# Beginning the first two FFN1 tiles on four pairs between the last score chunks, in a fused sigmoid attention and SwiGLU kernel

## The chip, the cores and the metric

The kernel runs on one core of a Trainium2 chip. The metric is device time in microseconds for one execution.

## The reference, cut to what matters

```python
# q, k, v: (8, 12, 448, 64)
scores = q @ k.T / 8 - log(448)
attn   = sigmoid(scores) @ v                 # "PV"
x      = attn as (3584, 768)
out    = (silu(x @ w_gate) * (x @ w_val)) @ w_out   # FFN1: w_gate, w_val (768, 1536); FFN2: w_out
```

The kernel works on quads of four heads; three quads give the x of one batch. x is held transposed as six "pairs" of 128 rows each (two pairs to a quad), and FFN1 sums over the six pairs. So the first FFN1 tile can be begun on pairs 0 to 3 while the third quad, quad 2, still lacks its last score chunks and its PV.

## The kernel before

Four accumulator tiles of two banks each form a ring; every score chunk, transpose, PV and FFN1 tile takes one. A score chunk is four 64x64 matmuls and one sigmoid on ScalarE (0.89 us from one to the next). FFN1 is one 128x128 matmul for each pair and bank: bank 0 gate, bank 1 value.

```python
def pv(n, how=0, at=None):
    ...                                     # 28 matmuls of 64x64 into P
    first = nc.vector.tensor_copy(out=x, in_=P[:, 0, :S])           # even pair, bank 0
    ...
    halves = [...]                                                  # odd pair, bank 1
    if how == 2:
        for o, i in halves:
            nc.scalar.copy(out=o, in_=i)    # waits for `first`
```

The stretch of the change. The comments give the ring tile by number:

```python
    chunk(2, 3)                             # tile 0
    chunk(2, 4)                             # tile 1, still being read by PV of quad 1
    chunk(2, 5)                             # tile 2

    k0 = ring_at[0] % 4                     # 3
    chunk(2, 6, at=(k0 + 1) % 4)            # tile 0
    early = [Banked("f", at=(k0 + i) % 4) for i in (0, 2)]      # tiles 3 and 1
    ffn1_mm(early[0], 0, 0, range(NP - 2))  # 8 matmuls
    ffn1_mm(early[1], 0, 1, range(2))       # 4
    pv(2, how=2, at=(k0 + 3) % 4)           # tile 2
    ffn1_mm(early[1], 0, 1, range(2, NP - 2))
    early.append(Banked("f", at=(k0 + 1) % 4))
    ffn1_mm(early[2], 0, 2, range(NP - 2))
    for f, Df in enumerate(early):
        ffn1_mm(Df, 0, f, range(NP - 2, NP))        # pairs 4 and 5, of quad 2
        ffn1_gate(Df, 0, f)
```

Of the kernel before, what the change touches and what calls it, by code (L numbers as in the profile page):

```python
# [19 lines left out]
def kernel(  # L20
# [10 lines left out]
    nc = tc.nc  # L31
    ctx.enter_context(tc.manual_schedule())

    B, H, S, D = q.shape
# [4 lines left out]
    NP = H // 2  # L39
# [74 lines left out]
    def apart(second, *firsts):  # L114

        for first in firsts:
            keys[0] += 1
            tc.add_to_no_dep_group(f"half{keys[0]}", first.ins)
            tc.declare_no_dep(second.ins, group=f"half{keys[0]}", reason="another bank or other partitions")


    FW = 3
    NW = NF // FW
    wg16 = [one.tile([128, NP, FW * 128], FP16, tag=f"wg{i}", name=f"wg16_{i}") for i in range(NW)]
    wv16 = [one.tile([128, NP, FW * 128], FP16, tag=f"wv{i}", name=f"wv16_{i}") for i in range(NW)]
# [93 lines left out]
    xT = {}  # L219

    def qk_tile(n, c, at=None):
        sd = Banked(at=at)
        sc = sd.t
        qt, kt = qT[(n, 0)], qT[(n, 1, c)]
        for w in range(2):
            for h2 in range(2):
                r = slice(h2 * 64, h2 * 64 + 64)
                nc.tensor.matmul(  # L228
                    out=sc[w * 64:(w + 1) * 64, h2, :S],
                    lhsT=kt[r, w * 64:(w + 1) * 64],  # L230
                    rhs=qt[r, :, w * 64:(w + 1) * 64],
                    start=True,
                    stop=True,
                )
        return sd

    def sig_tile(n, c, sd, split=False):
        sc = sd.t
        pt = ptp.tile([128, 2, S], FP16, tag="pt", name="pt")
        if split:  # L240
            for h2 in range(2):
                sd.read(
                    nc.scalar.activation(out=pt[:, h2, :], in_=sc[:, h2, :S], func=SIGM, bias=sb_t, scale=qkscale), h2  # L243
                )
        else:
            nc.scalar.activation(out=pt, in_=sc[:, :, :S], func=SIGM, bias=sb_t, scale=qkscale)  # L246
        pts[(n, c)] = pt

    def pv(n, how=0, at=None):

        b, j = divmod(n, NJ)
        P = Banked(at=at).t
        vt = v16.pop(n)
        for c in range(C):
            pt = pts.pop((n, c))
            for h2 in range(2):
                for w in range(2):
                    r = slice(w * 64, w * 64 + 64)
                    g = (w ^ h2) * 64
                    nc.tensor.matmul(  # L260
                        out=P[g:g + 64, h2, :S],
                        lhsT=vt[r, h2, c * D:(c + 1) * D],
                        rhs=pt[r, h2, :],
                        start=(c == 0),
                        stop=(c == C - 1),
                    )

        x = xtp.tile([128, S], FP16, tag="xT", name=f"xT_{b}_{2 * j}")
        first = nc.vector.tensor_copy(out=x, in_=P[:, 0, :S])  # L269
        xT[(b, 2 * j)] = x  # L270
        x = xtp.tile([128, S], FP16, tag="xT", name=f"xT_{b}_{2 * j + 1}")
        xT[(b, 2 * j + 1)] = x
        halves = [(x[w * 64:(w + 1) * 64, :], P[(1 - w) * 64:(2 - w) * 64, 1, :S]) for w in range(2)]
        done = [nc.vector.tensor_copy(out=o, in_=i) for o, i in halves[how:]]  # L274
        if how == 2:
            for o, i in halves:
                nc.scalar.copy(out=o, in_=i)

        def rest():
            if how == 1:  # L280
                o, i = halves[0]
                apart(nc.scalar.copy(out=o, in_=i), first, *done)

        return rest
# [1 line left out]

    hT = {}

    def ffn1_mm(D, b, f, prs):
        cs = slice((f % FW) * 128, (f % FW) * 128 + 128)  # L290
        for i, w16 in enumerate((wg16, wv16)):
            for pr in prs:
                D.write(
                    nc.tensor.matmul(  # L294
                        out=D.t[:, i, :S], lhsT=w16[f // FW][:, pr, cs], rhs=xT[(b, pr)],
                        start=(pr == 0), stop=(pr == NP - 1),
                    ),
                    i,
                )

    def ffn1(b, f):
        D = Banked("f", made=(b // 2, f))
        for prs in (range(NP - 2), range(NP - 2, NP)) if f == 0 else (range(NP),):
            ffn1_mm(D, b, f, prs)
        ffn1_gate(D, b, f)
        if b % 2:
            h_sums(b // 2, f)
            make_sums(2)
# [217 lines left out]
    for grp in visits:  # L526
        n, c = grp[0]
        b, j = divmod(n, NJ)
# [6 lines left out]
    def attn_step(group, pvs, how):  # L535
        for part in (group[:2], group[2:]):
            scs = [(n, c, qk_tile(n, c)) for n, c in part]
            rest = [pv(pvs.pop(0), how) for _ in range(len(pvs))]
            for i, (n, c, sc) in enumerate(scs):

                sig_tile(n, c, sc, split=len(group) == 4 and part[0] == group[0] and i == 1)
            for f in rest:
                f()
# [51 lines left out]
    def chunk(n, c, at=None):  # L595
        sig_tile(n, c, qk_tile(n, c, at))
# [22 lines left out]
    for c in range(3):  # L619
        chunk(1, c)  # L620
    pv(0)
    chunk(1, 3)
    chunk(1, 4)
# [9 lines left out]
    chunk(2, 0)  # L633
    chunk(2, 1)
    pv(1)
    chunk(2, 2)
    trans_pe(3)
# [3 lines left out]
    w_load("g", 3)  # L641
    w_load("v", 3)
    chunk(2, 3)
    chunk(2, 4)
    chunk(2, 5)

    k0 = ring_at[0] % 4
    chunk(2, 6, at=(k0 + 1) % 4)
    early = [Banked("f", at=(k0 + i) % 4) for i in (0, 2)]
    ffn1_mm(early[0], 0, 0, range(NP - 2))  # L650
    ffn1_mm(early[1], 0, 1, range(2))
    pv(2, how=2, at=(k0 + 3) % 4)
    ffn1_mm(early[1], 0, 1, range(2, NP - 2))
    early.append(Banked("f", at=(k0 + 1) % 4))
    ffn1_mm(early[2], 0, 2, range(NP - 2))
    for f, Df in enumerate(early):
        ffn1_mm(Df, 0, f, range(NP - 2, NP))
        ffn1_gate(Df, 0, f)
# [84 lines left out]
```

## Time and profile before

| | before |
|---|---|
| time, median of the first 3 runs | 416.99 us (416.38 to 417.77) |
| span of the profiled run | 415.2 us |
| TensorE busy | 97% |
| the stretch: from the scores of (2,3) to the first scores of the next visit | 21.61 to 34.46 = 12.85 us |
| gaps of TensorE in it | 0.52 and 0.32 us |

The rows of the profile are in the prediction. In a TensorE row, the first number is when the first matmul starts, but the second reaches to the end of the last one in the pipeline, so consecutive rows overlap; distances between starts are the safe reading.

### The profile page before, as it was taken

The numbers are of one execution on the slowest core, as the hardware profiler recorded it, in microseconds if no ns is written. First come the engines' busy times: TensorE is split into PE (matmuls) and PEld (weight loads), VectorE is DVE, ScalarE is ACT, GpSimd is POOL, SyncE is SP. The second block draws the span as 40 slices with busy tenths as digits, with TensorE's granted clock in tenths as the row PEclk, the third lists the DMA queues.
The fourth block names the chain that finished last, engine by engine and source line by source line (L and its number), as shares of the span: only waits on it lengthen the run. The fifth ranks groups of instructions, "written<-read, shape, count | busy, mean of one in ns | idle before, by whom it ended". The sixth has DMA issues, their size and how long they took to land.

```text
span 415.2 us, 7941 instructions
## 1 busy us (share of the span) xinstructions
PE 404.5 (97%) x3194; PEld 210.9 (51%) x3194; DVE 257.1 (62%) x472; ACT 213.4 (51%) x294; POOL 95.0 (23%) x125
## 2 busy tenths in 40 slices
PE   7899999999999999999999999999999999999995
PEld 3444544545555445445565445445555545555563
DVE  3637557779755555678654555568745447578653
ACT  5966985754444745845704865565715472222000
POOL 4528163345130553210030345020000000000000
PEclk9999999999999999999999999999999999999999
DMA  8999999996779995331275998330025400000135
GB/s 267 246 256 242 223 199 250 130 211 173 199 148 231 184 207 157 66 98 24 59 184 139 198 203 209 77 69 0 2 59 140 113 2 0 2 0 2 38 81 148
DMA packets 59845, 54.39 MB, mean 131 GB/s; under 512 B 35744, under 2 KB 53280, under 8 KB 59808
## 3 DMA queue, kind: packets, MB, share of 16 engines
q0 software_dynamic: 18880, 30.94, 34.3%
q1 hardware_dynamic: 40496, 22.62, 25.4%
q8 instruction: 25, 0.41, 0.4%
q10 hardware_dynamic: 432, 0.33, 0.3%
q14 instruction: 12, 0.10, 0.1%
HBM read 47.19 MB, written 11.01 MB: 140 GB/s over the span
## 4 chain that ended last, share of the span: by engine, by line
PE 87%; ACT 5%; DVE 4%; issue 2%; DMA 1%; SPq 0%; DVEq 0%; ACTq 0%
PE ps_D L294 49%; PE ps_D L418 18%; PE ps_D L228 8%; PE ps_D L260 6%; PE ps_D L476 6%; ACT pt L246 4%; DVE t L314 1%; DVE hT L318 1%; DMA st<-in_k_dram 1%; DVE S L377 1%; PE ps_D L198 1%; ACT s L312 0%; ACT pt L243 0%; SPq L149 0%; DVE T L204 0%
## 5 line engine op out<-in xcount | busy, mean ns | idle before, releaser
L246 ACT ACTIVATE pt<-ps_D,sb_t 128x896 f16<-128x896 f32 x148 | 140.2, 1016 | 83.4 <-PE ps_D L228 78.6
L294 PE MATMUL ps_D<-xT,wg 128*128 128x448 f16 x576 | 126.8, 353 | 0.1
L294 PE MATMUL ps_D<-xT,wv 128*128 128x448 f16 x576 | 126.4, 352 | 0.0
L314 DVE TENSOR_TENSOR t<-ps_D,s 128x448 f16<-128x448 f32 x96 | 59.7, 622 | 74.7 <-ACT s L312 74.4
L312 ACT ACTIVATE s<-ps_D 128x448 f16<-128x448 f32 x96 | 52.6, 548 | 83.4 <-PE ps_D L294 71.3
L294 PEld LDWEIGHTS <-wg 128*128 128x128 f16 x576 | 53.5, 98 | 58.3 <-issue 12.4
L294 PEld LDWEIGHTS <-wv 128*128 128x128 f16 x576 | 56.4, 98 | 52.6
L318 DVE SCALAR_TENSOR_TENSOR hT<-ps_D,t 128x448 f16<-128x448 f32 x96 | 60.0, 625 | 10.0
L179 POOL CAST c<-st 128x896 bf16<-128x896 f32 x41 | 38.5, 947 | 120.9 <-DMA T<-c 61.8
L228 PE MATMUL ps_D<-T,T 64*64 64x448 bf16 x644 | 44.2, 357 | 2.2 <-DVE T L204 0.8
L260 PE MATMUL ps_D<-pt,v 64*64 64x448 f16 x672 | 36.0, 349 | 0.4 <-ACT pt L246 0.3
L429 DVE TENSOR_SCALAR osb<-ps_D 128x384 f32<-128x384 f32 x43 | 24.0, 558 | 19.1 <-PE ps_D L418 18.1
L418 PEld LDWEIGHTS <-S 128*128 128x128 f16 x264 | 25.8, 98 | 17.1
L418 PE MATMUL ps_D<-wT,S 128*128 128x384 f16 x198 | 34.0, 326 | 0.0
L228 PEld LDWEIGHTS <-T 64*64 64x64 bf16 x644 | 15.0, 105 | 25.1 <-issue 19.0
L172 POOL DMA_DIRECT2D v<-in_v_dram x24 | 17.6, 731 | 44.3 <-PE ps_D L228 32.9
L269 DVE CAST xT<-ps_D 128x448 f16<-128x448 f32 x24 | 14.9, 622 | 19.7 <-PE ps_D L260 14.3
L435 DVE SCALAR_TENSOR_TENSOR osb<-ps_D,osb 128x384 f32<-128x384 f32 x33 | 18.4, 558 | 13.5 <-PE ps_D L418 13.5
L274 DVE CAST xT<-ps_D 64x448 f16<-64x448 f32 x42 | 26.1, 621 | 0.7
L260 PEld LDWEIGHTS <-v 64*64 64x64 f16 x672 | 19.8, 107 | 13.0 <-issue 1.6
L418 PEld LDWEIGHTS <-hT 128*128 128x128 f16 x198 | 18.9, 98 | 14.2 <-issue 2.1
L476 PE MATMUL ps_D<-wo,hT 128*128 128x384 f16 x144 | 24.2, 326 | 0.0
(45 smaller groups left out, 213.3 us busy)
## 6 DMA issues: line engine op xcount, KB each, us to landing
out_dram<-osb SPq DMA_DIRECT2D x52, 192.0 KB, 3.0
st<-in_q_dram POOLq DMA_DIRECT2D x20, 448.0 KB, 4.9
st<-in_k_dram POOLq DMA_DIRECT2D x20, 448.0 KB, 6.3
v<-in_v_dram POOLq DMA_DIRECT2D x24, 224.0 KB, 7.3
wg<-in_moe_w_gate_dram POOLq DMA_DIRECT2D x4, 576.0 KB, 11.9
wv<-in_moe_w_val_dram POOLq DMA_DIRECT2D x4, 576.0 KB, 13.0
wo<-in_moe_w_out_dram POOLq DMA_DIRECT2D x4, 576.0 KB, 9.8
st<-in_q_dram SPq DMA_DIRECT2D x3, 448.0 KB, 7.1
```

Of the source, the lines that this page charges most:

```text
L179: eng.tensor_copy(out=t.rearrange("p c h d -> p h c d"), in_=st.rearrange("p h (c d) -> p h c d", c=C))
L228: nc.tensor.matmul(out=sc[w * 64:(w + 1) * 64, h2, :S], lhsT=kt[r, w * 64:(w + 1) * 64], rhs=qt[r, :, w * 64:(w + 1) * 64], start=True, st ...
L246: nc.scalar.activation(out=pt, in_=sc[:, :, :S], func=SIGM, bias=sb_t, scale=qkscale)
L260: nc.tensor.matmul(out=P[g:g + 64, h2, :S], lhsT=vt[r, h2, c * D:(c + 1) * D], rhs=pt[r, h2, :], start=(c == 0), stop=(c == C - 1),)
L274: done = [nc.vector.tensor_copy(out=o, in_=i) for o, i in halves[how:]]
L294: nc.tensor.matmul(out=D.t[:, i, :S], lhsT=w16[f // FW][:, pr, cs], rhs=xT[(b, pr)], start=(pr == 0), stop=(pr == NP - 1),),
L312: D.read(nc.scalar.activation(out=s16, in_=D.t[:, 0, :S], func=SIGM), 0)
L314: D.read(nc.vector.tensor_tensor(out=t1, in0=D.t[:, 0, :S], in1=s16, op=MULT), 0)
L318: nc.vector.scalar_tensor_tensor(out=hT[(b // 2, f)][:, b % 2, :], in0=D.t[:, 1, :S], scalar=HSC, in1=t1, op0=MULT, op1=MULT),
L418: nc.tensor.matmul(out=D.t[:, bank, :hw], lhsT=l, rhs=B_(i), start=(first and i == 0), stop=(i == HF - 1), skip_group_check=True,),
L429: nc.vector.tensor_scalar(out=o, in0=D.t[:, bank, :hw], scalar1=HREC, scalar2=None, op0=MULT), bank
L476: nc.tensor.matmul(out=D.t[:, half, :hw], lhsT=h[:, m * 128:(m + 1) * 128], rhs=wo16[f // FW][:, f % FW, half * hw:(half + 1) * hw], start ...
```

## The change

The intent: fill the time in which TensorE waits for the sigmoids of quad 2 with FFN1 work that is ready, and let ScalarE's two PV copies start at once, as PV now has less work behind it to hide them.

```diff
             for o, i in halves:
-                nc.scalar.copy(out=o, in_=i)
+                apart(nc.scalar.copy(out=o, in_=i), first)
 ...
     chunk(2, 3)
-    chunk(2, 4)
-    chunk(2, 5)
     k0 = ring_at[0] % 4
-    chunk(2, 6, at=(k0 + 1) % 4)
-    early = [Banked("f", at=(k0 + i) % 4) for i in (0, 2)]
-    ffn1_mm(early[0], 0, 0, range(NP - 2))
-    ffn1_mm(early[1], 0, 1, range(2))
+    tile_of = lambda i: Banked("f", at=(k0 + i) % 4)
+    four = range(NP - 2)
+    chunk(2, 4, at=(k0 + 1) % 4)
+    early = [tile_of(0)]
+    ffn1_mm(early[0], 0, 0, four, (0,))      # gate only
+    chunk(2, 5, at=(k0 + 3) % 4)
+    ffn1_mm(early[0], 0, 0, four, (1,))      # value only
+    early.append(tile_of(2))
+    ffn1_mm(early[1], 0, 1, four, (0,))
+    chunk(2, 6, at=(k0 + 1) % 4)
+    ffn1_mm(early[1], 0, 1, four, (1,))
     pv(2, how=2, at=(k0 + 3) % 4)
-    ffn1_mm(early[1], 0, 1, range(2, NP - 2))
-    early.append(Banked("f", at=(k0 + 1) % 4))
-    ffn1_mm(early[2], 0, 2, range(NP - 2))
+    early.append(tile_of(1))
+    ffn1_mm(early[2], 0, 2, four)
```

`apart` tells the scheduler that the second instruction need not wait for the first. (`ffn1_mm` also takes a list of banks now; that line is cut.)

More of the change, by code (lines that the diff above doesn't have):

```diff
@@ L287, with ffn1_mm @@
     hT = {}
-    def ffn1_mm(D, b, f, prs):
+    def ffn1_mm(D, b, f, prs, banks=(0, 1)):
         cs = slice((f % FW) * 128, (f % FW) * 128 + 128)
-        for i, w16 in enumerate((wg16, wv16)):
+        for i in banks:
             for pr in prs:
@@ L294, in ffn1_mm @@
                     nc.tensor.matmul(
-                        out=D.t[:, i, :S], lhsT=w16[f // FW][:, pr, cs], rhs=xT[(b, pr)],
+                        out=D.t[:, i, :S], lhsT=(wg16, wv16)[i][f // FW][:, pr, cs], rhs=xT[(b, pr)],
                         start=(pr == 0), stop=(pr == NP - 1),
```

## The prediction

> **What bounds the kernel now.** I read the page first, for the engine shares and the chain that ended last; then the chain in order of time, to see whether the changed stretch (about 20 to 35 us) is on it; then the timelines of TensorE and ScalarE there; then the waits and the DMA issues. The page's chain first:
>
> ```profile
> PE 87%; ACT 5%; DVE 4%; issue 2%; DMA 1%; SPq 0%; DVEq 0%; ACTq 0%
> ```
>
> TensorE is the bound of the kernel as a whole. Time can be won here only where TensorE idles, or where it does more than the arithmetic needs. The TensorE timeline of the changed stretch (start, length, engine, line, operation, what ended the idle time before it):
>
> ```profile
> 20.71 0.94 PE L198 MATMUL ps_D<-idn,c 128*128 128x128 bf16 x14
> 21.61 0.38 PE L228 MATMUL ps_D<-T,T 64*64 64x448 bf16 x4
> 22.52 0.57 PE L228 MATMUL ps_D<-T,T 64*64 64x448 bf16 x8 [0.52 <-DVE xT L274]
> 23.41 0.38 PE L228 MATMUL ps_D<-T,T 64*64 64x448 bf16 x4 [0.32 <-ACT pt L246]
> 23.72 0.93 PE L294 MATMUL ps_D<-xT,wg 128*128 128x448 f16 x4
> ```
>
> L228 is the scores, four matmuls to a chunk. Counting tiles of the ring of four, the row at 21.61 is chunk (2,3), the one at 22.52 is (2,4) and (2,5) together, the one at 23.41 is (2,6). L294 is FFN1 and L260 is PV. There are two gaps, 0.52 and 0.32 us. From 23.41 on TensorE has no gap until about 45 us, as the chain shows (start, length, what):
>
> ```profile
> 22.24 1.13 ACT pt L246
> 23.36 0.04 issue
> 23.41 0.38 PE ps_D L228 x4
> 23.79 2.38 PE ps_D L294 x12
> 26.16 1.45 PE ps_D L260 x28
> 27.61 6.92 PE ps_D L294 x36
> 34.53 0.50 PE ps_D L228 x8
> 35.03 2.38 PE ps_D L294 x12
> ...
> 41.07 0.69 PE ps_D L228 x12
> ```
>
> Before 23.41 the pace is the sigmoid's. The ScalarE timeline holds thirteen of them back to back:
>
> ```profile
> 14.23 11.82 ACT L246 ACTIVATE pt<-ps_D,sb_t 128x896 f16<-128x896 f32 x13
> 28.39 1.06 ACT L277 CAST xT<-ps_D 64x448 f16<-64x448 f32 x2 [2.34 <-DVE xT L269]
> ```
>
> The last begins at 24.91 and ends at 26.05; they start 0.89 apart and last about 1.12 each. Counted back, the sigmoid of (2,2) ends at 22.46, of (2,3) at 23.36, of (2,4) at 24.25, of (2,5) at about 25.15. The second row is the two PV half copies, which begin only after VectorE's copy of the other bank has ended at 28.35.
>
> **What the Trainium skill says.** TensorEngine Tiling (Array Packing), section Key Properties: changing the tiling mode, not just the tile, drains TensorE. Scores and PV run as 64x64 tiles, FFN1 as the full array, so each passage from one to the other should cost something. The trace agrees: full-array blocks of 12 and 36 matmuls take 2.38 and 6.92 us, which is 0.189 each and 0.11 for the block; 64x64 blocks of 8 and 12 take 0.50 and 0.69, which is 0.0475 each and 0.12 for the block (28 then make 1.45, as PV does). TensorE: Matmul & The Clock Gate, section Step-by-step: matmuls stay in program order, only weight loads are pulled ahead; so a chunk that waits blocks the FFN1 work behind it, which is why the order of the program matters here. PSUM — Partial Sum Buffer, section PSUM bank collisions raise a hardware error: two engines on different banks run clean. The DVE copy takes bank 0 of PV's tile and ScalarE's halves take bank 1, so the wait that the change drops is not needed for safety; no run yet shows them side by side in this kernel.
>
> **The change part by part.** No instruction is removed or added: the same three chunks, 24 early FFN1 matmuls, 28 PV matmuls and five copies. What changes is the order on TensorE, the ring tile of each, and one dependency.
>
> Tiles. The start of the local numbering, k0, is now taken after chunk (2,3) instead of after (2,5), so it is ring tile 1 instead of 3. Chunk (2,4) goes to the tile of (2,2) and waits for that sigmoid (22.46), where it had waited for the last VectorE copy of PV of quad 1 (22.46 as well: the copy starts 21.84 and lasts 0.62). With the 0.05 us that other releases show it starts at about 22.51, as before at 22.52. So the first gap, 0.52 us, stays. The first FFN1 tile sits on the tile of that PV and is placed behind (2,4), so it can't fill it either. Chunk (2,5) waits for the sigmoid of (2,3), chunk (2,6) for that of (2,4); both orders keep a two-chunk distance.
>
> Order. I use the two laws above and check them on the kernel before. From 22.52: 8 score matmuls 0.50, to 23.02; wait to 23.41 (0.39); 4 scores 0.31, to 23.72; 12 FFN1 2.38, to 26.10; PV 1.45, to 27.55; 36 FFN1 6.92, to 34.47. The timeline's weight loads start at 23.72, 26.09, 27.54 and 34.46, so the laws hold within 0.01 us.
>
> After, from 22.51: (2,4) 0.31, to 22.82; gate of tile 0 on four pairs, 4 x 0.189 + 0.11 = 0.87, to 23.69; (2,5) 0.31, to 24.00, its sigmoid freed at 23.36, so no wait; eight FFN1 (value of tile 0, gate of tile 1) 1.62, to 25.62; (2,6) 0.31, to 25.93, freed at 24.25, no wait; four FFN1 0.87, to 26.80; PV 1.45, to 28.25; the remaining 32 FFN1 to the same point (eight of tile 2, twelve to close the three tiles, twelve of tile 3) 32 x 0.189 + 0.11 = 6.16, to 34.41.
>
> So the sum is 34.47 - 34.41 = 0.06 us won. Its terms: the gap filled, -0.39; one more score block, +0.12; two more full-array blocks, +0.22; the start, -0.01. The gap is filled, but the interleaving that fills it pays nearly all of it back in mode changes.
>
> ScalarE. Scores of (2,5) come at about 24.07, just where its slot was (24.02). Those of (2,6) come at about 26.0, so the last sigmoid moves from 24.91 to about 26.05 and ends at 27.15. PV needs it only for its last four matmuls, at 26.80 + 0.12 + 24 x 0.0475 = 28.06. Tile 2 of FFN1 on that ring tile comes at 28.25. So ScalarE's lost 1.1 us is off the path.
>
> PV copies. Before, PV's first copy began 0.18 us after the next weight load; so after, VectorE copies from 28.43 to 29.05. FFN1 asks for pair 4 at 28.25 + 0.11 + 8 x 0.189 = 29.87 and for pair 5 at 30.06. The halves on ScalarE take 1.06: in the old way from 29.09 to 30.15, late by about 0.1 to 0.15 us; at once, from 28.45 to 29.51, in time by half a microsecond. The dropped dependency is thus an insurance that the new order needs, not a gain over the kernel before, where the halves ended at 29.45 and were asked for at 30.0.
>
> DMA. The first gate and value weights, issued at 9.58 and 10.41:
>
> ```profile
> wg<-in_moe_w_gate_dram POOLq DMA_DIRECT2D x1, 576.0 KB, 10.3
> wv<-in_moe_w_val_dram POOLq DMA_DIRECT2D x1, 576.0 KB, 12.4
> ```
>
> They land at 19.9 and 22.8. The new order asks for them at 22.8 and 24.0, so neither is waited for.
>
> Downstream of 30 us the order of instructions is that of before, with the ring roles (PV, tile 0, tile 1, tile 2) in the same order, so the shift of 0.06 us should be carried to the end unchanged.
>
> **The rivals.** First: the mode changes are hidden, because the intercepts of my laws are drain that is there only at the end of a long block. Then the whole 0.39 us comes through, and the time would be 416.6. For it: the intent of the change. Against it: PV, between two FFN1 blocks, shows the 0.12 in full (1.45), and the two laws reproduce four block starts of the kernel before. Second: a short block costs more than the line says (I extrapolate from 12 full-array matmuls to 4), or the four-pair blocks meet a wait I haven't seen, such as the T copies of quad 3 that hold tile 1's ring tile (they end at 23.65; asked for at about 24.9) or a dependency of the changed tiles. At 0.1 to 0.3 us more for the three short blocks the time would be 417.1 to 417.3. Third: the first gap too is shortened, if (2,4) is released by the sigmoid a little sooner than by VectorE; by the starts above that is worth under 0.05 us. Fourth: the early sigmoids' new times change what GpSimd issues and when, and with it the later loads; the score chunks' inputs are long there and the chain has DMA only in its first 7 us, so this should be worth nothing.
>
> **Range and chances.** Predicted change -0.06 us, which no timing here resolves: the three runs before spread over 1.4 us (416.38 to 417.77). From the median, 416.99 - 0.06 = 416.9. The rivals reach from 416.6 to 417.3, and a median of a few runs wanders by some 0.4 either way, so I take 416.2 to 417.6 for 8 in 10. Two per cent are 8.3 us, more than the whole changed stretch could lose without an error: faster 0.005, same 0.99, slower 0.005.
>
> **What would show it right or wrong.** In the changed kernel's TensorE timeline there should be no gap after (2,4); the rows should alternate scores 4, FFN1 4, scores 4, FFN1 8, scores 4, FFN1 4, PV 28; PV should start at about 26.8 instead of 26.09, and the first scores of the next visit at 34.4 instead of 34.46. If these come at about 34.1, the mode change was free (first rival); if at 34.7, short blocks cost more (second). The gap before (2,4) should still be about 0.5. The sigmoids should show an idle time of about 1 us before the last, and the ScalarE halves should start with VectorE's copy. I am wrong if TensorE waits inside PV for the last sigmoid, or at FFN1's pair 5 for the halves, or if the time past 34.5 differs between the kernels by more than the shift.

## The result, and the profile after

The changed kernel took 416.60 us in the median of 6 runs (416.14 to 417.43); the kernel before, 416.84 in 6. The ratio is 0.9996, with a 95% interval of 0.9979 to 1.0012: the same. (A ratio is the mean time of one kernel's fast runs over that of the other's in the same rounds, so not quite the ratio of the medians quoted.)

The TensorE timeline of the changed kernel in the stretch; columns as before:

```profile
21.12 0.38 PE L228 MATMUL ps_D<-T,T 64*64 64x448 bf16 x4
22.02 0.38 PE L228 MATMUL ps_D<-T,T 64*64 64x448 bf16 x4 [0.52 <-ACT pt L246]
22.33 0.93 PE L294 MATMUL ps_D<-xT,wg 128*128 128x448 f16 x4
23.19 0.38 PE L228 MATMUL ps_D<-T,T 64*64 64x448 bf16 x4
23.51 0.93 PE L294 MATMUL ps_D<-xT,wv 128*128 128x448 f16 x4
24.27 0.92 PE L294 MATMUL ps_D<-xT,wg 128*128 128x448 f16 x4
25.12 0.38 PE L228 MATMUL ps_D<-T,T 64*64 64x448 bf16 x4
25.44 0.93 PE L294 MATMUL ps_D<-xT,wv 128*128 128x448 f16 x4
26.30 1.52 PE L260 MATMUL ps_D<-pt,v 64*64 64x448 f16 x28
27.75 0.93 PE L294 MATMUL ps_D<-xT,wg 128*128 128x448 f16 x4
```

The alternation: scores 4, FFN1 4, scores 4, FFN1 8, scores 4, FFN1 4, PV 28. One gap is left, 0.52 us before (2,4) at 22.02; the one of 0.32 us is gone. The next visit's scores start at 33.91, so the stretch is 33.91 - 21.12 = 12.79 us against 12.85. The profiled span is 0.5 us shorter than before, but (2,3), which precedes everything that was changed, already started 0.49 us sooner: that part is the scatter of the start, not the change.

ScalarE over the same time:

```profile
17.28 7.41 ACT L246 ACTIVATE pt<-ps_D,sb_t 128x896 f16<-128x896 f32 x8
25.62 1.01 ACT L246 ACTIVATE pt<-ps_D,sb_t 128x896 f16<-128x896 f32 x1 [0.93 <-PE ps_D L228]
27.87 1.06 ACT L277 CAST xT<-ps_D 64x448 f16<-64x448 f32 x2 [1.24 <-PE ps_D L260]
```

The last sigmoid starts after 0.93 us of idle time, and the two half copies start at 27.87, where VectorE's copy starts at 27.94: they lie side by side, and the runs below that keep this (e1, e3, e4, e5) are recorded as correct.

The chain of the changed kernel just behind the stretch (start, length, what) shows what a block costs besides its matmuls. It counts from the end of one block to the end of the next, so it has 33.98 where the timeline has 33.91:

```profile
33.98 0.50 PE ps_D L228 x8
34.48 2.38 PE ps_D L294 x12
36.86 0.50 PE ps_D L228 x8
37.36 0.89 PE ps_D L198 x14
38.25 2.27 PE ps_D L294 x12
40.52 0.69 PE ps_D L228 x12
```

Twelve FFN1 matmuls take 2.38 us behind scores (34.48) but 2.27 us behind the transposes of L198 (38.25). Those transposes use the full array, like FFN1. So the 0.11 us belongs to the passage from 64x64 tiles to the full array and not to "a new block".

What the 0.11 us is made of stays open. TensorE's weight loads (PEld) of the kernel before:

```profile
23.72 0.49 PEld L294 LDWEIGHTS <-wg 128*128 128x128 f16 x4 [0.20 <-issue]
24.30 0.67 PEld L294 LDWEIGHTS <-wv 128*128 128x128 f16 x4
```

The first load of the block starts together with its first matmul (23.72), while inside the block the first value weights are loaded 0.19 us ahead of their matmul (24.49). A load takes about 0.10 us (in the mean 98 ns for the 128x128 loads of L294, 105 and 107 ns for the 64x64 loads of L228 and L260), so a first load that nothing covers would look much like a drain of the array. No run tells the two apart; the cost of a passage is the same whichever it is.

### The profile page after: what moved, and what is told of

The parts are those of the page before. It is cut to its first block, busy times and chain, and to the rows that moved or that the text cites. A ratio compares the mean times of both kernels' runs of the same rounds, so it can differ in the third digit from the quotient of the medians.

```text
span 414.7 us, 7943 instructions
## 1 busy us (share of the span) xinstructions
PE 403.1 (97%) x3194; PEld 209.9 (51%) x3194; DVE 256.7 (62%) x472; ACT 213.5 (51%) x294; POOL 94.5 (23%) x125
## 4 chain that ended last, share of the span: by engine, by line
PE 89%; ACT 4%; DVE 3%; issue 2%; DMA 1%; POOL 0%; SPq 0%; DVEq 0%; ACTq 0%
PE ps_D L294 51%; PE ps_D L418 18%; PE ps_D L228 8%; PE ps_D L260 6%; PE ps_D L476 5%; ACT pt L246 3%; DMA st<-in_q_dram 1%; PE ps_D L198 1%; DVE S L377 1%; DVE t L314 1%; ACT s L312 0%; DVE hT L318 0%; ACT pt L243 0%; DVE T L204 0%; DVE xT L269 0%
## 5 line engine op out<-in xcount | busy, mean ns | idle before, releaser
L294 PE MATMUL ps_D<-xT,wg 128*128 128x448 f16 x576 | 126.6, 353 | 0.1
L294 PE MATMUL ps_D<-xT,wv 128*128 128x448 f16 x576 | 126.3, 352 | 0.0
L294 PEld LDWEIGHTS <-wg 128*128 128x128 f16 x576 | 53.5, 98 | 58.3 <-issue 12.4
L294 PEld LDWEIGHTS <-wv 128*128 128x128 f16 x576 | 56.2, 98 | 52.6 <-issue 0.4
L318 DVE SCALAR_TENSOR_TENSOR hT<-ps_D,t 128x448 f16<-128x448 f32 x96 | 60.0, 625 | 10.0
L228 PE MATMUL ps_D<-T,T 64*64 64x448 bf16 x644 | 44.4, 357 | 2.6 <-DVE T L204 1.2
L260 PE MATMUL ps_D<-pt,v 64*64 64x448 f16 x672 | 36.0, 349 | 0.4 <-ACT pt L246 0.3
L228 PEld LDWEIGHTS <-T 64*64 64x64 bf16 x644 | 15.0, 105 | 25.6 <-issue 19.3
L260 PEld LDWEIGHTS <-v 64*64 64x64 f16 x672 | 19.8, 107 | 13.0 <-issue 1.0
L476 PE MATMUL ps_D<-wo,hT 128*128 128x384 f16 x144 | 24.2, 326 | 0.3 <-DVE osb L489 0.3
```

Source lines behind the costliest of these rows:

```text
L228: nc.tensor.matmul(out=sc[w * 64:(w + 1) * 64, h2, :S], lhsT=kt[r, w * 64:(w + 1) * 64], rhs=qt[r, :, w * 64:(w + 1) * 64], start=True, st ...
L260: nc.tensor.matmul(out=P[g:g + 64, h2, :S], lhsT=vt[r, h2, c * D:(c + 1) * D], rhs=pt[r, h2, :], start=(c == 0), stop=(c == C - 1),)
L294: nc.tensor.matmul(out=D.t[:, i, :S], lhsT=(wg16, wv16)[i][f // FW][:, pr, cs], rhs=xT[(b, pr)], start=(pr == 0), stop=(pr == NP - 1),),
L318: nc.vector.scalar_tensor_tensor(out=hT[(b // 2, f)][:, b % 2, :], in0=D.t[:, 1, :S], scalar=HSC, in1=t1, op0=MULT, op1=MULT),
L476: nc.tensor.matmul(out=D.t[:, half, :hw], lhsT=h[:, m * 128:(m + 1) * 128], rhs=wo16[f // FW][:, f % FW, half * hw:(half + 1) * hw], start ...
```

## The experiments

"Rest" is the span less the end of the stretch, that is, everything behind it.

| run | what | stretch, expected | stretch, measured | rest |
|---|---|---|---|---|
| before | | | 12.85 | 380.7 |
| changed | | 12.79 | 12.79 | 380.8 |
| e1_apart_only | before, halves let loose | 12.85 | 12.85 | 380.6 |
| e2_no_apart | changed, halves wait | 12.9 to 13.05 | 13.04 | 382.6 |
| e3_merged | changed, two passages fewer | 12.56 to 12.66 | 12.79 | 382.0 |
| e4_split1 | changed, two passages more | 13.02 | 13.03 | 381.9 |
| e5_split3 | changed, six passages more | 13.48 | 13.48 | 380.4 |
| e6_one_fill | before, one block moved | 12.70 | 12.71 | 382.4 |
| e7_both_gaps | both gaps filled | 12.20 to 12.5 | 12.31 | 380.7 |
| e8_pairs | e7, (2,5) beside (2,6) | 12.08 | 12.78 | 382.3 |
| e9_wo_later | before, a later load | 12.85 | 12.85 | 380.9 |
| e10_both | e8 and e9 | 12.08 | 12.54 | 382.0 |

### The halves alone, and the order alone

```diff
# e1: kernel before
-                nc.scalar.copy(out=o, in_=i)
+                apart(nc.scalar.copy(out=o, in_=i), first)
# e2: changed kernel
-                apart(nc.scalar.copy(out=o, in_=i), first)
+                nc.scalar.copy(out=o, in_=i)
```

> The kernel before, with only the halves of PV on ScalarE let loose from VectorE's copy. The measure of all these runs is the stretch on TensorE from the four scores of chunk (2,3) to the eight scores of the next visit: 12.85 us before (21.61 to 34.46), 12.79 changed (21.12 to 33.91). Theory (the order of TensorE alone makes the time, the halves are off its path): the halves start with VectorE's copy, some 0.7 us sooner, and the stretch stays 12.85 within 0.03. Rival (the small gain of the change came from the halves): the stretch falls by about 0.05 or more.

Measured: the halves started at 28.33, 0.12 us behind the first FFN1 matmul after PV (28.21), where in the kernel before that distance is 0.84; and the stretch did not move (22.28 to 35.13). Letting them loose alone wins nothing.

> The changed kernel, with the halves waiting for VectorE's copy again. Theory of the prediction: the new order leaves only eight FFN1 matmuls behind PV, so the second of pair 5's halves comes late. From the changed trace the halves would end 28.60 + 1.06 = 29.66, and pair 5 is asked for at 29.46: TensorE waits some 0.15 to 0.25 us at pair 5 and the stretch grows from 12.79 to 12.9 to 13.05, so the change without it would be slower than before in this stretch. Rival (the dropped dependency is no part of the result): the stretch stays 12.79 within 0.03.

Measured: 21.38 to 34.42 = 13.04. TensorE where FFN1 tile 0 asks for pairs 4 and 5, and ScalarE's halves:

```profile
29.54 0.79 PE L294 MATMUL ps_D<-xT,wg 128*128 128x448 f16 x2
30.17 0.54 PE L294 MATMUL ps_D<-xT,wv 128*128 128x448 f16 x2
```

```profile
28.86 1.06 ACT L277 CAST xT<-ps_D 64x448 f16<-64x448 f32 x2 [1.97 <-DVE xT L269]
```

Two such matmuls take 0.54 in every other row; here the pair takes 0.79, so 0.25 us is spent waiting for halves that end at 28.86 + 1.06 = 29.92. The new order needs the dropped dependency: without it the change would cost 0.19 us instead of winning 0.06.

### More passages

```diff
# e4: changed kernel; pv() calls mid[c] ahead of its chunk c
-    ffn1_mm(early[1], 0, 1, four, (1,))
-    pv(2, how=2, at=(k0 + 3) % 4)
+    ffn1_mm(early[1], 0, 1, range(2), (1,))
+    pv(2, how=2, at=(k0 + 3) % 4, mid={3: range(2, 4)})
# e5
+    ffn1_mm(early[1], 0, 1, range(1), (1,))
+    pv(2, how=2, at=(k0 + 3) % 4, mid={2: range(1, 2), 4: range(2, 3), 6: range(3, 4)})
```

> The changed kernel with the four value matmuls of tile 1 split two and two, the second two put after 12 of the 28 matmuls of PV. Same instructions, same tiles, no new wait (the gap of TensorE is already filled, and the last sigmoid ends before PV's last chunk needs it), but two more passages between full-array and 64x64 matmuls. Theory (each passage costs 0.11 to 0.12 us): the stretch grows by 0.23, from 12.79 to 13.02. Rival (passages are free, the constant of a block is an artefact of long blocks or of waits): 12.79 within 0.03.

> As the run before, but the four value matmuls of tile 1 lie singly: one ahead of PV, one after each of its first 8, 16 and 24 matmuls, so six more passages than in the changed kernel. Theory (cost per passage, whatever the length of the block): the stretch grows by 6 x 0.115 = 0.69, from 12.79 to 13.48. Rival a (free): 12.79. Rival b (the line doesn't hold down to blocks of one matmul, a short block costs more): over 13.6.

Measured: 13.03 and 13.48, so 0.24 us for two passages and 0.69 for six, 0.115 to 0.12 each. The TensorE timeline of e5 inside PV:

```profile
25.61 0.36 PE L296 MATMUL ps_D<-xT,wv 128*128 128x448 f16 x1
25.91 0.57 PE L262 MATMUL ps_D<-pt,v 64*64 64x448 f16 x8
26.41 0.36 PE L296 MATMUL ps_D<-xT,wv 128*128 128x448 f16 x1
26.70 0.57 PE L262 MATMUL ps_D<-pt,v 64*64 64x448 f16 x8
27.21 0.36 PE L296 MATMUL ps_D<-xT,wv 128*128 128x448 f16 x1
27.50 0.57 PE L262 MATMUL ps_D<-pt,v 64*64 64x448 f16 x8
```

One full-array matmul between two 64x64 blocks occupies 25.91 - 25.61 = 0.30 us, of which the matmul itself is 0.19; eight PV matmuls occupy 0.50, of which 0.38 is their own. No row shows a wait. The rival that passages are free falls, and so does the one that short blocks cost more than the line says: it holds from 36 matmuls down to one.

### One block moved

```diff
# e6: kernel before
-    chunk(2, 6, at=(k0 + 1) % 4)
-    early = [Banked("f", at=(k0 + i) % 4) for i in (0, 2)]
-    ffn1_mm(early[0], 0, 0, range(NP - 2))
+    early = [Banked("f", at=k0)]
+    ffn1_mm(early[0], 0, 0, range(NP - 2))
+    chunk(2, 6, at=(k0 + 1) % 4)
+    early.append(Banked("f", at=(k0 + 2) % 4))
```

> The kernel before with one move: the eight matmuls of FFN1 tile 0 stand ahead of the scores of (2,6) instead of behind them; tiles as before. The wait before (2,6), 0.39 us, shrinks to about 0.13 (tile 0 now waits for the first T copy of quad 3), and only one more full-array block is made (+0.11, its score block stays single). Theory: the stretch (12.85 before, 12.79 changed) becomes 12.70. Rival (fills are worth their full wait): 12.59. Rival (what is filled is always paid back): 12.85.

Measured: 21.61 to 34.32 = 12.71. A single moved block wins 0.14 us, more than twice what the change wins, with two passages more than the kernel before where the change has four more. So the same gap is worth more with fewer passages, even though 0.15 us of it is left: FFN1 starts at 23.17, where the laws without a wait make 23.02.

### Fewer passages

```diff
# e3: changed kernel
     early = [tile_of(0)]
-    ffn1_mm(early[0], 0, 0, four, (0,))
+    ffn1_mm(early[0], 0, 0, four)
     chunk(2, 5, at=(k0 + 3) % 4)
-    ffn1_mm(early[0], 0, 0, four, (1,))
     early.append(tile_of(2))
-    ffn1_mm(early[1], 0, 1, four, (0,))
+    ffn1_mm(early[1], 0, 1, four)
     chunk(2, 6, at=(k0 + 1) % 4)
-    ffn1_mm(early[1], 0, 1, four, (1,))
```

> The changed kernel with the same tiles but longer blocks: (2,4), all eight of FFN1 tile 0, (2,5), all eight of tile 1, (2,6) directly ahead of PV. Two passages fewer than in the changed kernel. Theory (0.115 per passage): the stretch falls by 0.23 from 12.79 to 12.56; the last sigmoid comes later, so PV's last four matmuls may wait up to 0.1: 12.56 to 12.66. Rival (passages free): 12.79 or a little more. The whole time moves by 0.05 per cent at most, under what rounds resolve: same.

Measured: 21.27 to 34.06 = 12.79, a miss; by this number alone the rival (passages free) looks right. The inside of the trace says otherwise. ScalarE's last sigmoid, and the weight loads of PV's last chunk (PEld):

```profile
26.53 1.01 ACT L246 ACTIVATE pt<-ps_D,sb_t 128x896 f16<-128x896 f32 x1 [0.93 <-PE ps_D L228]
```

```profile
27.59 0.11 PEld L260 LDWEIGHTS <-v 64*64 64x64 f16 x3 [0.29 <-issue]
```

The sigmoid ends at 27.54 and the last chunk of PV begins at 27.59, after an idle time. From (2,6) at 26.03 to the FFN1 behind PV at 27.90 is 1.87 us, where 32 matmuls of 0.0475 and one passage make 1.64. So the saved 0.23 us of passages turned into 0.23 us of waiting for the sigmoid: with no FFN1 between (2,6) and PV, nothing covers it. I had allowed it 0.1. The whole time was 417.02 us in the median against 417.72, ratio 0.9992 (0.997 to 1.0014): the same, as expected.

### Both gaps

```diff
# e7: e3, with PV of quad 1 tracked by bank (in pv(); cut: DP is its tile)
+        if n == 1:
+            DP.read(first, 0)
+            for ins in done:
+                DP.read(ins, 1)
 ...
+    early = [tile_of(0)]
+    ffn1_mm(early[0], 0, 0, range(3), (0,))       # pairs 0 to 2, gate, ahead of (2,4)
     chunk(2, 4, at=(k0 + 1) % 4)
-    early = [tile_of(0)]
-    ffn1_mm(early[0], 0, 0, four)
+    ffn1_mm(early[0], 0, 0, four, (1,))
+    ffn1_mm(early[0], 0, 0, range(3, 4), (0,))
     chunk(2, 5, at=(k0 + 3) % 4)
```

A first form, with the gate of pair 3 ahead of the value matmuls, was unsafe: that matmul had lost its wait for the copy that writes pair 3. Behind the value matmuls, which wait for the same copy, it is safe.

> A version meant to beat both: as the run before, and also three gate matmuls of tile 0 (pairs 0 to 2) ahead of (2,4), in the first gap, which the change left open. For this the reads of PV of quad 1 are tracked by bank, so that bank 0 of that tile, free since about 21.2, can be written while its other bank is still being copied. Working on the times of the kernel before: (2,3) to 21.92, three FFN1 to 22.60, (2,4) to 22.91, five FFN1 to 23.96, (2,5) to 24.27, eight FFN1 to 25.89, (2,6) to 26.20, PV to 27.65, 32 FFN1 to 33.81. The stretch becomes 12.20 if the value weights, landing at 22.8, are there at 22.9, and up to 12.5 if they or the last sigmoid are waited for. Theory: 12.20 to 12.5, and the start of the next visit moves by the same; at the end of the kernel at most 0.6 us are left, since a VectorE-bound stretch lies at 80 to 103 us that may keep part of it. Rival (mode changes or waits eat it): 12.79. Whole time: ratio to before 0.9985 to 0.9995 on a mean, not clear of noise.

Measured: 22.14 to 34.45 = 12.31, 0.54 us less than before, and both gaps gone. Its chain inside PV:

```profile
26.50 0.31 PE ps_D L228 x4
26.81 1.14 PE ps_D L261 x24
27.95 0.04 issue
27.98 0.38 PE ps_D L261 x4
```

The chain itself breaks PV at its last four matmuls, which start at 27.98, right after the sigmoid's end (26.92 + 1.01 = 27.93). Again 1.86 us stands in place of 1.64. (My working for it made 12.20 where the laws make 12.08: it counted a passage between (2,6) and PV, which are of one mode. With the wait added to the right sum, 12.08 + 0.22 = 12.30. So the hit at 12.31 is in part luck: the wait that the range allowed for makes up for the wrong sum.) The whole time was 417.28 us in the median against 417.72, ratio 0.9995 (0.9975 to 1.0015): not clear of noise.

```diff
# e8: e7
+    early.append(tile_of(2))
+    ffn1_mm(early[1], 0, 1, range(1), (0,))
     chunk(2, 5, at=(k0 + 3) % 4)
-    early.append(tile_of(2))
-    ffn1_mm(early[1], 0, 1, four)
     chunk(2, 6, at=(k0 + 1) % 4)
+    ffn1_mm(early[1], 0, 1, range(1, 4), (0,))
+    ffn1_mm(early[1], 0, 1, four, (1,))
```

> The version that filled both gaps, with chunks (2,5) and (2,6) next to each other ahead of most of tile 1, so that the last sigmoid has 1.43 us of FFN1 in front of PV and PV no longer waits for it (it waited 0.24 us in that version and in the merged one). The number of passages stays. Theory: the stretch falls from 12.31 by that wait, to 12.08; PV takes 1.45 again. Rival (the 0.24 in PV were not the sigmoid): 12.31. At the end of the kernel 0.7 us less than before at best, if nothing later waits.

Measured: 21.27 to 34.05 = 12.78. PV takes 1.45 again (26.44 to 27.89), so the 0.24 was the sigmoid. But the stretch lost more than that elsewhere:

```profile
22.25 0.38 PE L228 MATMUL ps_D<-T,T 64*64 64x448 bf16 x4
23.27 0.93 PE L299 MATMUL ps_D<-xT,wv 128*128 128x448 f16 x4 [0.63 <-DMA wv<-in_moe_w_val_dram]
```

The first value matmul should have come 0.31 us after 22.25, at 22.56; it came at 23.27, when the value weights had landed: 0.71 us late. Without that the stretch is 12.07, as the laws say. In e10, which has the same order of the stretch, the same wait took 0.46 us (23.38 instead of 22.92) and the stretch was 12.54, again 12.08 without it. The whole time was 416.20 in the median of the five fast runs (417.15 with the slow one counted in) against 417.52, ratio of fast runs 0.9976 (0.9945 to 1.0006): the same, not settled either.

This also qualifies e7. It asks for the value weights 1.30 us behind the scores of (2,3), just as e8 does. In e7's one trace they landed at about 22.1 (issued at 10.58, 11.5 us on their way) and were asked for at 23.44; in e8 they landed at about 23.2 and were asked for at 22.56. So the 12.31 against 12.78 doesn't rank the two orders: e7 had the earlier load and a stretch that began 0.87 us later, and with the times of e8 it would have waited too.

### What scatters behind the stretch

The "rest" column has two groups, 380.4 to 380.9 and 381.9 to 382.6, and they don't follow the stretch. In all six traces of the longer group, and in none of the shorter, the scores of quad 6 wait for a transposing DMA, by 0.70 to 1.32 us, which is most of the 1.5 us between the groups. Here it is in e10:

```profile
63.42 0.57 PE L228 MATMUL ps_D<-T,T 64*64 64x448 bf16 x8 [0.89 <-DMA T<-c]
```

```diff
# e9: kernel before; e10: e8
-        (5, 4): ((fetch, 7), (w_out, 0)),
-        (6, 0): ((ready, 7), (w_out, 1)),
+        (5, 4): ((fetch, 7),),
+        (6, 0): ((ready, 7), (w_out, 0), (w_out, 1)),
```

> The kernel before with nothing changed in the stretch; only the load of the first quarter of the output weights is issued after the casts of quad 7 instead of before them. In four of the nine traces so far the scores of quad 6 wait 0.7 to 1.3 us at about 63 us for a transposing DMA, whatever the kernel's stretch, and those are the four longest spans (416.1 to 417.0). Theory (that DMA shares the engines with the loads issued at its side, so one load fewer lets it land sooner): no such wait, spans 414.5 to 415.5, times 416.2 to 417.2, no run over 417.5; mean ratio to before 0.998 to 0.9995. Rival (the wait comes from the load of the keys landing late, not from the traffic beside the transpose): the wait and the long runs stay. The stretch stays 12.85.

> Both: the stretch of the paired version and the later load. Theory: stretch 12.08, no wait for the transposing DMA, ratio to before 0.997 to 0.9985. Rival (TensorE's earlier start only turns into a wait for a load further on, since the loads of the first 60 us keep their own pace): stretch 12.08 and a DMA wait at about 62 us that returns what was won.

Measured: e9 showed no such wait in its profile, but one of its six runs took 418.6 us; median 417.24 against 417.52, ratio 0.9994 (0.997 to 1.0018). e10 had the later load and the wait all the same, 0.89 us; median 417.95, ratio 0.9991 (0.9961 to 1.0021). So my theory, that this load makes the transpose late, falls. What makes the transpose land late in six of the twelve traces stays open. The length of the stretch doesn't decide it (12.79 without in the changed kernel, 12.79 with in e3; 12.31 without, 12.78 with).

## Why the prediction was right

**TensorE bound, two laws, the sum.** Right, term by term. Shifted by the 0.49 us of the earlier start, the changed trace has the starts at 22.82, 23.68, 24.00, 25.61, 25.93, 26.79, 28.24 and 34.40; the prediction had 22.82, 23.69, 24.00, 25.62, 25.93, 26.80, 28.25 and 34.41. It predicted 0.06 us won, and 12.85 - 12.79 = 0.06 was. The new order repeats: in the changed kernel PV starts 5.18 us behind the scores of (2,3), in e2 5.19. The gap that was filled and the passages that pay it back are both shown: the gap by the timelines, the passages by e4 and e5. The prediction counted a constant for each block; counted by passages, which the runs support, the same sum reads: TensorE was free of the scores of (2,5) at 22.52 + 8 x 0.0475 = 22.90 and idle to 23.41, 0.51 us; the new order has eight passages from (2,4) on instead of four, 4 x 0.115 = 0.46; the difference is 0.05.

**First rival, mode changes hidden.** Wrong, as it was given: 2 and 6 more of them cost 0.24 and 0.69 us. That TensorE keeps the order of its matmuls, on which the prediction rests, fits the traces: e6 shows that FFN1 tile 0 could start at 23.17, and in the kernel before, with (2,3) and (2,4) at the same times, TensorE idled until (2,6) at 23.41 with that FFN1 behind it.

**Second rival, short blocks dearer, or an unseen wait.** Wrong for the changed kernel. Such waits are what befell the variants that went further, through the last sigmoid (e3, e7) and the value weights (e8, e10).

**First gap.** Right: 0.52 us before and after, with ScalarE in place of VectorE as the engine that ends it. e7 showed that it can be filled.

**PV copies as an insurance.** Right in kind, shown by e1 (no gain alone) and e2. The size was off: the prediction had the halves late by 0.1 to 0.15 us, and e2 measured 0.25. It had put the block's 0.11 us ahead of its matmuls, so that pair 5 was asked for too late: the timelines have it at the end, in front of the next block (FFN1 behind PV starts at 27.75 and asks for pair 4 at 29.27, 8 x 0.19 later).

**Last sigmoid off the path.** Right: it ended at 26.63, and PV ran at its 1.45 us. The same slip is in the prediction's 28.06 for PV's last four matmuls, which should be 27.94; it was harmless there.

**"So the shift of 0.06 us should be carried to the end unchanged."** This was not shown. In the two profiled runs it was carried as far as about 94 us, where the two TensorE timelines lie 94.07 - 93.52 = 0.55 apart, the start's 0.49 and the 0.06. Then both kernels wait for VectorE, but at different places. The kernel before waits ahead of the scores at 96.03 (its chain comes there from VectorE's hT, L318), and the distance grows to 0.89. The changed kernel waits ahead of the 48 matmuls of L476, and it falls to 0.48. The kernel before:

```profile
102.89 0.76 PE L228 MATMUL ps_D<-T,T 64*64 64x448 bf16 x12
103.59 7.97 PE L476 MATMUL ps_D<-wo,hT 128*128 128x384 f16 x48
```

The changed kernel:

```profile
102.00 0.76 PE L228 MATMUL ps_D<-T,T 64*64 64x448 bf16 x12
103.11 7.96 PE L476 MATMUL ps_D<-wo,hT 128*128 128x384 f16 x48 [0.35 <-DVE osb L489]
```

Behind them, at PV, the distance is 111.89 - 111.40 = 0.49, which is the start's scatter alone. So in these two runs nothing of the 0.06 us reached the end; as the rest scatters by 0.5 us even among the traces without the DMA wait, two runs can't settle it. Nor is that stretch the same from run to run: VectorE's sums there (L377) take 0.36 us or up to about 1. GpSimd and VectorE of the kernel before, at one such place:

```profile
93.42 1.09 POOL L179 CAST c<-st 128x896 bf16<-128x896 f32 x1 [2.17 <-DMA st<-in_q_dram]
```

```profile
93.36 0.36 DVE L377 TENSOR_TENSOR S<-hT,hT 128x384 f16<-128x384 f16 x1
93.75 0.97 DVE L377 TENSOR_TENSOR S<-S,hT 128x384 f16<-128x384 f16 x1
```

The long sum begins inside a GpSimd cast and ends soon after it. It is so at every long sum of L377 in the traces of both kernels: five in the one and six in the other begin inside a cast, take 0.43 to 1.08 us and end 0.20 or 0.21 us behind the cast; all others begin outside one and take at most 0.4 us. The Trainium skill, SBUF — State Buffer, section SBUF: two separate sides, says that a VectorE operation with two SBUF inputs and a GpSimd operation that reads SBUF exclude each other on a shared port; the traces agree at all eleven. But no run took the casts away, so as a cause of the scatter of the whole time it is argued, not shown.

**The time.** 416.9 was predicted and 416.6 measured, inside the range of 416.2 to 417.6. A hit of this kind is no evidence by itself, since no runs here tell 0.06 us from nothing, and the range covered every rival too; what carries it is the stretch.

## What to carry to other kernels

Before filling a gap of TensorE with other work, count the passages between tiling modes that the filling adds: here each cost 0.115 us, and four more of them ate 0.46 of the 0.51 us won. Fill a gap with one long block rather than with slices on both sides of every wait (e6 won 0.14 us in the stretch with one move), and join blocks of one mode only as long as something still covers the wait behind them (e3). When a fill works, look at once for the next wait: the dependency that must go with it (e2), the sigmoid (e7) or the load (e8) that becomes the bound.

## What the Trainium skill lacked or had wrong

- TensorEngine Tiling (Array Packing), section Key Properties, says that changing the tiling mode drains TensorE, and gives no figure. Here a passage costs 0.11 to 0.12 us either way, whether the block holds 1 or 36 matmuls (0.69 us for six passages), and nothing between transposes and FFN1, both of the full array. Whether drain or the first weight load makes up this time isn't shown.
- No page that I read says that a dependency between two readers of different banks of one accumulator tile, kept by the scheduler, can itself make TensorE wait. Here it was worth 0.25 us (e2), and none in the other order (e1).
